# Turning attention rows on VectorE inside the attention instead of on TensorE during the first routing

## The chip, the cores and the metric

The kernel runs on one core of one Trainium2 chip. The metric is the device time of one execution in microseconds (us). The core has five engines that work side by side and wait for one another through semaphores: TensorE (PE in the profile, its weight loads PEld), VectorE (DVE), ScalarE (ACT), GpSimd (POOL) and SyncE (SP), which here only issues transfers (DMAs) and reads a register.

## The reference

An attention with sigmoid in place of softmax, and behind it a mixture of experts in which each token goes to one expert. All inputs are float32.

```python
# q, k, v: (8 batches, 12 heads, 448 tokens, 64)
scores = scale * np.matmul(q, k.transpose(0, 1, 3, 2)) - np.log(S)
attn = 1.0 / (1.0 + np.exp(-scores))
out = np.matmul(attn, v)
# x: (3584 tokens, 768): the heads of a token side by side
x = np.ascontiguousarray(out.transpose(0, 2, 1, 3)).reshape(B * S, H * D)
# experts: N=3584, D=768, E=8, F=1024, cap = N // E = 448 tokens each
logits = x @ w_gate
flat = logits.flatten()
for idx in np.argsort(-flat):                 # best (token, expert) first
    tok, e = (int(idx) // E, int(idx) % E)
    if assigned[tok] >= 0 or counts[e] >= cap:
        continue
    assigned[tok] = e
    counts[e] += 1
    ...
for e in range(E):
    h = np.maximum(x[assigned == e] @ w1[e], 0.0)
    out[assigned == e] = h @ w2[e]
```

## The kernel before

**Attention.** The work is cut into 48 pairs of heads, `(b, pr)` with 8 batches of `NP` = 6 pairs. One turn of the main loop takes a current pair, prepares the next and finishes the old one, and the order of the code is the order on each engine's queue:

1. In every even turn `load` issues the DMAs of two pairs, the fourth and fifth ahead: k and v on SP's queue, q on POOL's. The tiles `nkq` have four buffers, so a load waits until an older tile was turned.
2. `turn(nxt)` (L408) makes `kqT` on VectorE with a transpose of 32x32 blocks (128x896 elements); `split` copies it to `kqH` on ScalarE (L416) and takes the rest `kqL` on VectorE (L417).
3. `scores` (L433) runs on TensorE in three pieces `c`, each followed by a sigmoid on ScalarE (L423) into `at`. The split stands behind the first of the three.
4. `av(old)` (L457, and L463 for odd pairs) multiplies by v on TensorE into PSUM tiles `tp`, of which there are two. VectorE copies the result into `xt` (L465), for odd pairs with an addition (L467). An odd pair takes both `tp` tiles.
5. In even turns `rest_scores` (L443) handles the last 64 tokens of the next pair and the current one.
6. One item of the list `bg` is done: `logits(b)` (L478, TensorE, with an addition on VectorE, L480), or a piece of `rows`.

`XT[b]` holds a batch's attention output with the features on partitions: partition p of pair r is feature 128r + p, and the 448 tokens lie along the free dimension. The experts need whole token rows in the DRAM tensor `xs`, because a token's row is gathered by index. `rows(b, c, hf, eng)` makes them: for 112 tokens and three pairs it does three TensorE transposes into a `tp` tile (L489), copies that to `xr` on ScalarE (L492) or VectorE (L494), and with the second half stores 112 rows of 3072 bytes through SP (L496). A batch takes eight calls. Batch 0's calls go through `bg` during the attention; those of the last `LATE` = 7 batches go to the list `late`, and so `XT` has seven buffers.

**First routing.** Eight times, one expert after the other takes its 448 tokens (`Router.phase`): `keys` on VectorE, a `search` in 16 steps for the threshold, then `pick`, `place` and `lists`. In the first routing a step of the search counts on VectorE (L178), sums over partitions with one small TensorE matmul (L190), and makes the next thresholds on VectorE (L202, L215, L217). Nothing of the experts can run before this routing has picked the first expert and listed its tokens. Between its steps the code puts the late rows: one call before `R.start`, seven behind `keys`, three behind each step of the search. Then `actx.close()` releases the attention's SBUF.

**Experts.** For expert kx, `gather` fetches the tokens' rows from `xs` by an indirect DMA of POOL (L625), `xturn` transposes them on TensorE in blocks of 128 tokens and 128 features (L639: the rows are the stationary operand, the identity streams), and ScalarE and VectorE split them into `xh` and `xl` (L642, L643). Every expert has 24 such transposes, in eight groups of three. Weights come through SP (L592, L596) and are split into `wh` and `wl`; the products are done in three matmuls each (L734 to L738 and L771 to L775). The other routings run beside the experts' matmuls. The experts with kx of 6 and 7 load some weights with a step of two elements (`slice(d2, 256, 2)`, L764) and turn their results on VectorE (L669).

Of the kernel before, what the change touches and what calls it, by code (L numbers as in the profile page):

```python
# [7 lines left out]
F32 = mybir.dt.float32  # L8
# [11 lines left out]
BIG = 16384.0  # L20
TWO23 = float(2 ** 23)
XR_BUFS = 12
LATE = 7
XT_BUFS = 7
XA_BUFS = 5
AT_BUFS = 8
YT_BUFS = 3
# [312 lines left out]
def moe_attention(tc, q, k, v, w_gate, w1, w2, out):  # L340
    nc = tc.nc
    B, H, S, D = q.shape
    DM = H * D
    E, _, F = w1.shape
    CP, NCH, NP, ND, NF = 112, S // 112, H // 2, DM // 128, F // 128
    G4 = 4
    PSUM = bass.MemoryType.PSUM
    with contextlib.ExitStack() as ctx:
# [10 lines left out]
        xa = actx.enter_context(tc.tile_pool(name="xa", bufs=1))  # L359

        xs = dr.tile([B * S, DM], F32, name="xs")
# [9 lines left out]
        def load(b, g, qq=(nc.gpsimd, nc.gpsimd), vq=nc.sync):  # L371


            nat["v", b, g] = ld.tile([128, G4, 3, D], F32, name="nv", bufs=3)
            nat["r", b, g] = ld.tile([128, 2, D], F32, name="nr", bufs=3)
            for i in range(2):
                t = nat["kq", b, 2 * g + i] = ld.tile([128, 2, S // 32, 32], F32, name="nkq", bufs=4)
                for n, (qn, src) in enumerate(((nc.sync, k), (qq[i], q))):
                    for j in range(2):
                        rws = src[b, g * G4 + 2 * i + j].rearrange("(c p) (x d) -> x p c d", p=32, x=2)  # L380
                        for x in range(2):
                            o = 64 * j + 32 * x
                            qn.dma_start(t[o:o + 32, n], rws[x])  # L383
            vs = v[b, g * G4:(g + 1) * G4]
            for h in range(G4):
                vq.dma_start(nat["v", b, g][:, h], vs[h, :384].rearrange("(c p) d -> p c d", p=128))
            for i in range(2):
                vq.dma_start(nat["r", b, g][HI if i == 0 else LO],
                             vs[2 * i:2 * i + 2, 384:].rearrange("h p d -> p h d"))
# [56 lines left out]
        XT = {}  # L446

        def av(b, pr, end=False):


            if pr == 0:
                XT[b] = xa.tile([128, NP, S], F32, name="xt", bufs=XT_BUFS)
            p = ps_t.tile([128, 512], F32, name="tp")
# [18 lines left out]
        def logits(b, prs):  # L472

            s, g = b % 4, b // 4
            p = ps_t.tile([128, 512], F32, name="tp")
            for pr in prs:
                for c in range(NCH):
                    nc.tensor.matmul(p[32 * c:32 * c + 32, :CP], wgz[:, pr, s, :], XT[b][:, pr, c * CP:(c + 1) * CP],  # L478
                                     start=(pr == prs[0]), stop=(pr == prs[-1]))
            nc.vector.tensor_tensor(LE[:, g], LE[:, g], p[:, :CP], OP.add)  # L480

        XR = {}

        def rows(b, c, hf, eng):
            if hf == 0:
                XR[b] = xa.tile([CP, DM], F32, name="xr", bufs=XA_BUFS)
            p = ps_t.tile([128, 512], F32, name="tp")
            for i in range(3):
                nc.tensor.transpose(p[:CP, i * 128:(i + 1) * 128], XT[b][:, hf * 3 + i, c * CP:(c + 1) * CP], ident)  # L489
            dst = XR[b][:, hf * 384:(hf + 1) * 384]  # L490
            if eng == "act":
                nc.scalar.copy(dst, p[:CP, :384])  # L492
            else:
                nc.vector.tensor_copy(dst, p[:CP, :384])  # L494
            if hf == 1:
                nc.sync.dma_start(xs[b * S + c * CP:b * S + (c + 1) * CP], XR[b])  # L496

        pairs = [(b, pr) for b in range(B) for pr in range(NP)]
        NPR = len(pairs)
        turn(*pairs[0], ((0, 1), (1, 2)))()  # L500
        bg, late = [], []
        consts = route_consts(nc, cp, K)
        for i in range(NPR + 1):
            cur = pairs[i] if i < NPR else None
            nxt = pairs[i + 1] if i + 1 < NPR else None
            old = pairs[i - 1] if i else None
            if cur and cur[1] % 2 == 0:
                nx = i // 2 + 2
                if nx < NPR // 2:
                    load(nx // 3, nx % 3)  # L510
            split = turn(*nxt) if nxt else None
            for c in range(3 if cur else 0):
                scores(*cur, c)
                if c == 0 and split:
                    split()
            if bg and not cur:
                bg.pop(0)()
            if old:
                av(*old, not cur)
            if cur and cur[1] % 2 == 0:  # L520
                rest_scores(*nxt)
            if i > 2:
                next(consts, None)
            if bg and cur:
                bg.pop(0)()
            if old == (B - 1, NP - 2):
                bg.append(lambda: logits(B - 1, range(NP - 2)))
            if old and old[1] == NP - 1:
                b = old[0]
                if b < B - 1:  # L530
                    bg.append(lambda b=b: logits(b, range(NP)))
                for c in range(NCH):
                    for hf in range(2):
                        if b >= B - LATE:
                            late.append(lambda b=b, c=c, hf=hf: rows(b, c, hf, "act"))
                        else:
                            bg.append(lambda b=b, c=c, hf=hf: rows(b, c, hf, "dve"))
        for f in bg:
            f()
        logits(B - 1, [NP - 2, NP - 1])  # L540
# [76 lines left out]
        xg, XH = {}, {}  # L617
# [10 lines left out]
        def xturn(kx, j, n, hf, wide):  # L628
            if (j, hf) == (0, 0):
                XH[kx] = (xp.tile([128, ND, S], F32R, name="xh", bufs=2),  # L630
                          xp.tile([128, ND, S], F32R, name="xl", bufs=2))
            xh, xl = XH[kx]
            if wide and hf:
                p = ps_s.tile([128, 2, 512], F32, name="sc")[:, 0]
            else:
                p = ps_t.tile([128, 512], F32, name="tp")
            for i in range(3):
                dd = hf * 3 + i
                nc.tensor.transpose(p[:, i * n:(i + 1) * n], xg[kx, j][:n, dd * 128:(dd + 1) * 128], ident[:n, :n])  # L639
            pv = p[:, :3 * n].rearrange("p (a t) -> p a t", a=3)  # L640
            sl = (slice(None), slice(hf * 3, hf * 3 + 3), slice(j * 128, j * 128 + n))
            nc.scalar.activation(xh[sl], pv, AF.Copy)  # L642
            nc.vector.tensor_tensor(xl[sl], pv, xh[sl].bitcast(F32), OP.subtract)  # L643
# [172 lines left out]
        for kx in range(E):  # L816
# [21 lines left out]
            for step, cost in enumerate(moe(kx)):  # L838
                clock[0] += cost
                t = clock[0]  # L840
# [7 lines left out]
                if t >= t_chore:  # L848
                    c = next((c for c in chores if c[0] <= t), None)
# [37 lines left out]
```

## Time and profile before

| what | value |
|---|---|
| median of 3 runs | 882.02 us (881.35 to 885.34) |
| profiled execution, its own time | 883.43 us |
| its span | 881.7 us |
| mean granted TensorE clock | 0.987 |
| attention (to about 277 us) | TensorE busy throughout from 44 us on |
| first routing (277 to about 320 us) | VectorE busy 35.5 of 43 us, TensorE 30.8 |
| experts (340 to 870 us) | TensorE busy 524 of 530 us |

A line of a group of instructions reads: code line, engine, operation, output<-inputs, shape, number; then busy microseconds in all, mean nanoseconds of one, and the idle time of the engine just before them with what ended it. A line of the chain of waits reads: start, duration, engine, tile, line. A line of a timeline reads: start, duration, engine, line, operation, and in brackets the engine's idle time before it and who ended that. A line of a windows table gives the stretch, its width, the busy time of each engine shown with the number of instructions, the granted clock, the share of the DMA engines and GB/s.

### The profile page before, as it was taken

What the parts mean: (1) busy time and instruction counts of PE and PEld (TensorE: products, weight loads), DVE (VectorE), ACT (ScalarE), POOL (GpSimd) and SP (SyncE); (2) the same over time, 40 slices, a digit from 0 to 9 for tenths busy, and PEclk for the clock granted to TensorE, in tenths of its full rate; (3) what the DMA queues carried; (4) which work ended last, traced back from release to release, by engine and by line L of the source; (5) the groups of instructions that cost most, each with busy time, mean ns of one, the idle gap of its engine ahead of it and who ended that gap; (6) DMA issues with size and microseconds to landing.
All of it is one profiled execution on the core that took longest, in us unless ns stands there. A gap on an engine that the chain in (4) does not pass through costs nothing.

```text
span 881.7 us, 16211 instructions
## 1 busy us (share of the span) xinstructions
PE 840.1 (95%) x5467; PEld 636.9 (72%) x5467; DVE 542.4 (62%) x2060; ACT 447.3 (51%) x612; POOL 466.0 (53%) x446
## 2 busy tenths in 40 slices
PE   6999999999999739998999999999999999999996
PEld 3455555555554528987988988988888888999996
DVE  4566555555554988958859879779779631332130
ACT  6777677777775734434434434534434344541420
POOL 9744344444410014854864873873883883851561
PEclk9999999999999979998999999999999999999999
DMA  9866766666621855443442442551542542634643
GB/s 173 165 142 149 153 126 127 127 126 127 126 43 54 270 192 154 120 138 123 128 136 97 160 155 81 177 162 57 189 153 72 170 153 90 209 96 141 203 151 126
DMA packets 213811, 122.16 MB, mean 139 GB/s; under 512 B 153344, under 2 KB 202496, under 8 KB 213728
## 3 DMA queue, kind: packets, MB, share of 16 engines
q1 hardware_dynamic: 200992, 87.62, 38.2%
q0 software_dynamic: 10880, 33.28, 12.0%
q8 instruction: 43, 0.70, 0.3%
q10 hardware_dynamic: 1856, 0.23, 0.2%
q14 instruction: 40, 0.33, 0.1%
HBM read 96.76 MB, written 24.31 MB: 137 GB/s over the span
## 4 chain that ended last, share of the span: by engine, by line
PE 82%; DVE 11%; issue 2%; DMA 2%; POOL 1%; SPq 1%; ACT 1%; POOLq 0%; DVEq 0%; ACTq 0%
PE tp L457 13%; PE sc L433 11%; PE sc L736 9%; PE sc L734 9%; PE sc L738 9%; PE sc L773 6%; PE sc L775 6%; PE sc L771 6%; DVE r_junk L178 4%; PE tp L463 2%; PE sc L443 2%; PE tp L639 2%; PE tp L652 2%; PE tp L478 1%; PE rt L289 1%
## 5 line engine op out<-in xcount | busy, mean ns | idle before, releaser
L605 POOL TENSOR_TENSOR wl<-wr,wh 128x768 fp32r<-128x768 f32 (+1 forms) x96 | 204.9, 2145 | 124.5 <-ACT wh L603 116.8
L423 ACT ACTIVATE at<-sc,bias 128x896 f32<-128x896 f32 x168 | 161.5, 1006 | 67.1 <-PE sc L443 38.4
L383 POOL DMA_DIRECT2D nkq<-in_q_dram x188 | 118.4, 646 | 116.2 <-DVE kqT L408 104.6
L775 PE MATMUL sc<-hh,wl 128*128 128x448 f32 (+2 forms) x400 | 150.2, 375 | 0.0
L738 PE MATMUL sc<-xh,wl 128*128 128x448 f32 (+2 forms) x396 | 146.2, 369 | 0.0
L736 PE MATMUL sc<-xl,wh 128*128 128x448 f32 (+2 forms) x396 | 146.0, 369 | 0.1
L773 PE MATMUL sc<-hl,wh 128*128 128x448 f32 (+2 forms) x400 | 145.5, 364 | 0.2 <-POOL hl L746 0.2
L734 PE MATMUL sc<-xh,wh 128*128 128x448 f32 (+2 forms) x396 | 145.0, 366 | 0.0
L771 PE MATMUL sc<-hh,wh 128*128 128x448 f32 (+2 forms) x400 | 144.1, 360 | 0.4 <-issue 0.4
L178 DVE TENSOR_SCALAR_CACHE_REDUCE r_junk<-r_KE,r_T 128x224 bf16<-128x224 f32 x315 | 123.2, 441 | 0.1
L603 ACT ACTIVATE wh<-wr 128x768 fp32r<-128x768 f32 (+1 forms) x112 | 102.0, 939 | 36.3 <-DMA wr<-in_moe_w_dram 23.4
L457 PE MATMUL tp<-at,nv 128*64 128x448 f32 x576 | 118.8, 548 | 0.0
L746 POOL TENSOR_TENSOR hl<-yt,hh 128x896 fp32r<-128x896 f32 x32 | 68.4, 2136 | 48.8 <-ACT yt L745 47.2
L742 ACT ACTIVATE hh<-sc 128x896 fp32r<-128x896 f32 x32 | 29.5, 921 | 117.1 <-PE sc L738 117.1
L417 DVE TENSOR_TENSOR kqL<-kqT,kqH 128x896 fp32r<-128x896 f32 (+1 forms) x49 | 52.5, 1073 | 58.5 <-ACT kqH L416 58.4
L773 PEld LDWEIGHTS sc<-hl,wh 128*128 128x128 f32 x400 | 75.8, 189 | 6.8 <-issue 1.1
L625 POOL DMA_INDIRECT xr<-xs,r_idx x32 | 32.0, 999 | 91.2 <-ACT wh L603 80.2
L736 PEld LDWEIGHTS sc<-xl,wh 128*128 128x128 f32 x396 | 75.2, 190 | 6.7 <-issue 0.5
L457 PEld LDWEIGHTS tp<-at,nv 128*64 128x64 f32 x576 | 37.1, 136 | 59.1 <-issue 56.6
L734 PEld LDWEIGHTS sc<-xh,wh 128*128 128x128 f32 x396 | 75.2, 190 | 6.0
L771 PEld LDWEIGHTS sc<-hh,wh 128*128 128x128 f32 x400 | 76.0, 190 | 4.8 <-issue 0.6
L738 PEld LDWEIGHTS sc<-xh,wl 128*128 128x128 f32 x396 | 75.1, 190 | 5.3
(166 smaller groups left out, 1266.1 us busy)
## 6 DMA issues: line engine op xcount, KB each, us to landing
wr<-in_moe_w_dram SPq DMA_DIRECT2D x64, 384.0 KB, 3.0
wr<-in_moe_w_dram SPq DMA_DIRECT2D x48, 512.0 KB, 3.6
nkq<-in_k_dram SPq DMA_DIRECT2D x192, 56.0 KB, 2.6
xs<-xr SPq DMA_DIRECT2D x32, 336.0 KB, 3.3
nkq<-in_q_dram POOLq DMA_DIRECT2D x188, 56.0 KB, 2.7
nv<-in_v_dram SPq DMA_DIRECT2D x92, 96.0 KB, 2.7
ys<-yt SPq DMA_DIRECT2D x20, 112.0 KB, 1.9
nr<-in_v_dram SPq DMA_DIRECT2D x46, 32.0 KB, 2.2
```

The costliest lines, as they stand in the source:

```text
L178: nc.vector.tensor_scalar(junk, KE, T[:, i:i + 1].bitcast(F32), None, OP.is_ge, OP.add, accum_out=cnt[:, i:i + 1])
L383: qn.dma_start(t[o:o + 32, n], rws[x])
L423: nc.scalar.activation(a, p[:, :, :S], AF.Sigmoid, bias=bias, scale=1 / math.sqrt(D))
L457: nc.tensor.matmul(p[j * 64:j * 64 + 64, :S], nat["v", b, g][:, h0 + j, c, :], AT[b, pr, c][:, j, :], start=(c == 0), stop=(c == 2 and pr ...
L603: nc.scalar.activation(hi, raw[u], AF.Copy)
L605: eng.tensor_tensor(lo, raw[u], hi.bitcast(F32), OP.subtract)
L734: nc.tensor.matmul(ph[:, f, lo:hi], wh[:, a, fs], xh[:, dd, lo:hi], start=st, stop=False)
L736: nc.tensor.matmul(ph[:, f, lo:hi], wh[:, a, fs], xl[:, dd, lo:hi], start=False, stop=False)
L738: nc.tensor.matmul(ph[:, f, lo:hi], wl[:, a, fs], xh[:, dd, lo:hi], start=False, stop=en)
L771: nc.tensor.matmul(py[:, d2, :w], wh[:, a, dsl], h1, start=st, stop=False)
L773: nc.tensor.matmul(py[:, d2, :w], wh[:, a, dsl], h2, start=False, stop=False)
L775: nc.tensor.matmul(py[:, d2, :w], wl[:, a, dsl], h1, start=False, stop=(j == 1 and a == 3))
```

## The change

- `rows` is now used for the last batch alone (`LATE` = 1): eight calls, one before `R.start` and seven behind `keys`; nothing is put between the steps of the search any more. Batch 0's rows leave the attention as well.
- A new function `turn_rows` does batches 0 to 6. After each odd pair an item goes into `bg` that transposes two pairs (128x896 elements) in blocks of 32x32 on VectorE, in one instruction. Three such items make a batch, 21 in all; the logits of a batch come behind the third. Its output `xz` is [128, 14, 32, 6]: the six pairs lie innermost, so the instruction writes with a step of six elements (24 bytes).
- With the third item SP stores the batch in four DMAs, one for 32 partitions, each of 32x14 pieces of 192 elements (768 bytes). A row of `xs` now holds feature 128r + p at column 6p + r.
- `rows` writes its copy on ScalarE with the same step of six, so that batch 7 has that order too.
- `xturn` takes the columns `dd::NP`, every sixth element of a gathered row, as the stationary operand of its transposes.
- `XT` has three buffers in place of seven; `xz` has two.

```diff
-LATE = 7
-XT_BUFS = 7
+LATE = 1
+XT_BUFS = 3
+XZ_BUFS = 2
...
-        def rows(b, c, hf, eng):
+        def rows(b, c, hf):
...
-            dst = XR[b][:, hf * 384:(hf + 1) * 384]
-            if eng == "act":
-                nc.scalar.copy(dst, p[:CP, :384])
-            else:
-                nc.vector.tensor_copy(dst, p[:CP, :384])
+            dst = XR[b].rearrange("p (c r) -> p r c", r=NP)[:, hf * 3:hf * 3 + 3]
+            nc.scalar.copy(dst, p[:CP, :384].rearrange("p (r c) -> p r c", r=3))
...
+        def turn_rows(b, pr):
+
+            if pr == 1:
+                XR[b] = xa.tile([128, S // 32, 32, NP], F32, name="xz", bufs=XZ_BUFS)
+            nc.vector.transpose(XR[b].rearrange("p i j r -> p r i j")[:, pr - 1:pr + 1],
+                                XT[b][:, pr - 1:pr + 1].rearrange("p r (i t) -> p r i t", t=32))
+            if pr == NP - 1:
+                for a in range(4):
+                    nc.sync.dma_start(xs[b * S:(b + 1) * S, 192 * a:192 * a + 192].rearrange("(i t) c -> t i c", t=32),
+                                      XR[b][32 * a:32 * a + 32].rearrange("t i j r -> t i (j r)"))
...
+            if old and old[1] % 2 and old[0] < B - LATE:
+                bg.append(lambda b=old[0], pr=old[1]: turn_rows(b, pr))
             if old and old[1] == NP - 1:
                 b = old[0]
                 if b < B - 1:
                     bg.append(lambda b=b: logits(b, range(NP)))
-                for c in range(NCH):
+                for c in range(NCH if b >= B - LATE else 0):
                     for hf in range(2):
-                        if b >= B - LATE:
-                            late.append(lambda b=b, c=c, hf=hf: rows(b, c, hf, "act"))
-                        else:
-                            bg.append(lambda b=b, c=c, hf=hf: rows(b, c, hf, "dve"))
+                        late.append(lambda b=b, c=c, hf=hf: rows(b, c, hf))
...
-                nc.tensor.transpose(p[:, i * n:(i + 1) * n], xg[kx, j][:n, dd * 128:(dd + 1) * 128], ident[:n, :n])
+                nc.tensor.transpose(p[:, i * n:(i + 1) * n], xg[kx, j][:n, dd::NP], ident[:n, :n])
```

## The prediction, made before the changed kernel ran

> **What bounds the kernel now.** I read the page's first part, then a table of windows by stage, then the chain of waits and the timeline inside the stages that the change touches.
>
> ```profile
> PE 840.1 (95%) x5467; PEld 636.9 (72%) x5467; DVE 542.4 (62%) x2060; ACT 447.3 (51%) x612; POOL 466.0 (53%) x446
> ...
> 44.00:105.00 61.00, 61.00 (x520) 32.16 (x514) 38.06 (x70) 42.94 (x47) 25.09 (x40) 1.00 0.72 150
> 105.00:277.00 172.00, 172.00 (x1450) 86.91 (x1450) 92.23 (x112) 125.88 (x138) 65.26 (x104) 1.00 0.52 106
> 277.00:320.00 43.00, 30.75 (x216) 19.23 (x216) 35.48 (x202) 26.50 (x57) 0.00 (x0) 0.99 0.70 225
> 340.00:870.00 530.00, 524.29 (x2913) 466.29 (x2912) 338.02 (x1605) 213.01 (x320) 325.82 (x211) 0.99 0.43 135
> ```
>
> The window rows give, after the width, the busy time of PE, PEld, DVE, ACT and POOL, then the granted clock, the DMA share and GB/s. The attention (to 277 us) and the experts (from 340) are bound by TensorE, which is busy for the whole of two windows and 524 of 530 us of the other. The first routing (277 to 320) is not: there VectorE is busy 35.5 of 43 us. So a microsecond taken off TensorE counts in the attention and in the experts, and in the routing only if the row work there stands in VectorE's way. The profiled execution took 883.43 us, span 881.7; the median of the three timed runs is 882.02, 1.4 us less.
>
> **The row transposes that go.** By windows of line 489 alone (PE and PEld busy), and by the chain:
>
> ```profile
> 44.00:105.00 61.00, 4.31 (x24) 2.36 (x24) 1.00 0.72 150
> 276.00:320.00 44.00, 27.52 (x168) 16.74 (x168) 0.99 0.68 220
> by line: PE tp L457 39.4%; PE sc L433 35.3%; PE tp L463 7.5%; PE sc L443 7.4%; PE tp L489 6.6%; PE tp L478 4.3%
> ```
>
> Batch 0's 24 transposes run between 44 and 105 us, and the third row is the chain of that window: L489 is 6.6% of 61 us, 4.0 us, all on the path. **Term 1: -4.0 us.** Batch 0's eight VectorE copies (L494) go too, off the path.
>
> The other 168 run in the routing; 24 of them (batch 7) stay. The 144 that go, with 48 ACT copies, look large. The chain there:
>
> ```profile
> 290.71 0.04 issue
> 290.75 0.18 PE rt L190
> ...
> 290.95 0.18 DVE r_j L202 x2
> ...
> 291.15 0.16 DVE r_T L215
> 291.31 0.13 DVE r_J L217
> 291.44 1.11 DVE r_junk L178 x6
> ...
>   DVE r_j L202: 0.5, 2
> ```
>
> One search step takes 1.85 us, nearly all VectorE. Its TensorE instruction starts 0.04 us after the last count although row transposes stand around it in PE's queue; over 16 steps r_j waited for it 0.5 us in all (last row). So taking the late rows away gives the search nothing: term 0. (The stores that these rows feed: next fence.)
>
> **What the routing may lose.** With no row work TensorE idles through the search:
>
> ```profile
> 316.00:318.00 2.00, 0.00 (x0) 0.00 (x0) 1.79 (x7) 0.00 (x0) 0.00 (x0) 1.00 0.73 240
> 318.00:320.00 2.00, 0.59 (x3) 0.35 (x3) 1.46 (x9) 0.00 (x0) 0.00 (x0) 0.78 0.02 6
> 320.00:322.00 2.00, 0.00 (x0) 0.10 (x1) 1.90 (x5) 0.00 (x0) 0.00 (x0) 0.50 0.45 151
> L190 PE MATMUL rt<-r_cnt,c_G x16: 164/164/164, 286.4 to 314.8; 128*128 128x3 bf16 x16
> L167 PE MATMUL rt<-ident,r_KT x14: 257/269/368, 284.1 to 648.7; 112*128 112x112 f32 x14
> ```
>
> The last two columns, DMA share and GB/s, show the late stores through by 318 us (240 GB/s, then 6), before the first weights start: they hold up nothing either. The granted clock is still 1.00 just after the row transposes and 0.50 from 320. After the change it should fall near 290. L167's slowest against its usual, 368 to 269 ns, is my bound for a cold matmul, 1.4 times; so L190 may cost up to 66 ns more, 16 times: 0 to +1.1 us. **Term 2: +0.5.** The Trainium skill (TensorE: Matmul & The Clock Gate, Part 4) says that transposes do not count as busy for the clock, so that it would be low here already and this term zero; the 1.00 above, with little but transposes on PE, speaks against it. By its formulas for a single matmul (same page, Single matmul latency) a cold L190 is 185 ns for 167 warm, an estimate of 0.3 us over 16.
>
> Batch 7's eight ACT copies now write every sixth element. In the chain three of them (0.49 us each) alternate with transposes ahead of the keys' transpose:
>
> ```profile
> 282.52 0.49 ACT xr L492
> 283.06 1.04 PE tp L489 x6
> 284.13 0.42 PE rt L167 x2
> ```
>
> Free if such writes cost nothing; at 1.68 times the streaming part (below) some 0.2 us each, over five or six copies about 1.2. **Term 3: +0.4**, nearer the free end: no scattered ACT write is in the trace.
>
> **The turn on VectorE.** 21 block transposes of 128x896, three a batch, each right after an even pair's xt copy and ahead of the next kqT:
>
> ```profile
> L408 DVE STREAM_TRANSPOSE kqT<-nkq 128x896 f32<-128x896 f32 x47 | 51.8, 1103 | 2.5 <-DMA nv<-in_v_dram 1.5 <-DMA nkq<-in_k_dram 0.2
> L408 DVE STREAM_TRANSPOSE kqT<-nkq 128x448 f32<-128x448 f32 x2 | 1.2, 624 | 5.7 <-DMA nkq<-in_k_dram 5.7
> L669 DVE STREAM_TRANSPOSE yt<-sc 128x896 f32<-128x896 f32 x5 | 5.6, 1118 | 32.5 <-PE sc L775 25.0 <-issue 7.5
> L151 DVE TENSOR_REDUCE rt<-ML 112x32 f32<-112x256 f32 x7 | 4.2, 605 | 0.2
> 175.06 1.10 DVE L408 STREAM_TRANSPOSE kqT<-nkq 128x896 f32<-128x896 f32 x1
> 177.23 1.09 DVE L417 TENSOR_TENSOR kqL<-kqT,kqH 128x896 fp32r<-128x896 f32 x1 [1.08 <-ACT kqH L416]
> 179.87 0.62 DVE L465 COPY xt<-tp 128x448 f32<-128x448 f32 x1 [1.55 <-PE tp L463]
> 180.71 1.91 ACT L423 ACTIVATE at<-sc,bias 128x896 f32<-128x896 f32 x2 [1.71 <-PE sc L443]
> ```
>
> The first two rows make a transpose 145 ns and 1.07 ns per element. L669, the same operation writing every second element (8 bytes apart), takes 1118. The new one writes 24 bytes apart, a step that no row has. L151 reads SBUF at 64 bytes apart: (605-145)/256 = 1.80 ns per element, 1.68 times the dense rate. So one turn costs 1.1 to 145+896x1.80 = 1760 ns. Its cover is the idle time behind the delayed kqT: VectorE idles 1.55 us before the odd pair's copy, ACT 1.71 us before the next sigmoid but one. All of 1.1 hides and 1.76 nearly; without that cover 21 turns would cost 23 to 37 us. I take 1.1 to 1.2, since L669 is nearest. What queues behind a turn: kqT, then kqH and two sigmoids on ACT, then scores of the next pair. The logits of batches 0 to 6 move one pair later, behind an odd pair that uses both tp banks, so they wait for that copy (0.62 us, in the fence): 0 to 7 x 0.62 = 4.3 us. TensorE has the next pair's rest scores to do meanwhile, so I take a tenth: **term 4: +0.5**.
>
> **DMA.** Batch by batch, four stores of 32x14 pieces of 768 bytes replace four of 112 of 3072: the same 336 KB and the same count of 32 in all, 28 now inside the attention. A batch's 1.4 MB in 33 us is 42 GB/s; at the routing's 225 GB/s for a share of 0.70 that adds 0.13 to the attention's 0.52 to 0.72, or 0.26 if smaller pieces halve the rate.
>
> ```profile
> SPq L496 <- DVE xr L494: 10.3, 4, 3.3
> nkq<-in_k_dram SPq DMA_DIRECT2D x112, 56.0 KB, 2.5
> ```
>
> On SP the next k and v loads queue behind a store that waits for the turn. Batch 0's four stores did just that (10.3 us of SP waiting) and PE showed no gap from 44 to 105 us; loads land 2.5 us after issue, and the code issues them for the fourth and fifth pair ahead. POOL's q loads and gathers pass nothing. Zero; without the lead each store wait would cost up to 3.3 us, seven times.
>
> **The experts' transposes.** All 192 now load their stationary operand at a step of 24 bytes:
>
> ```profile
> 340.00:870.00 530.00, 26.69 (x168) 19.30 (x168) 0.99 0.43 135
> L639 PEld LDWEIGHTS tp<-ident,xr 128*128 128x128 f32 x135 | 16.9, 144 | 15.0 <-DVE xl L643 6.5 <-issue 5.1 <-DMA xr<-xs,r_idx 0.9
> L478 PEld LDWEIGHTS tp<-xt,wgz 128*32 128x32 f32 x384 | 8.9, 110 | 7.3 <-DVE kqL L417 3.5 <-ACT xt L465 1.6 <-issue 1.4
> L771 PEld LDWEIGHTS sc<-hh,wh x97: 186/188/192, 399.8 to 543.6; 128*128 128x128 f32 x97
> L771 PEld LDWEIGHTS sc<-hh,wh x62: 193/194/195, 782.7 to 849.7; 128*128 128x128 f32 x62
> 526.26 0.49 PE L639 MATMUL tp<-ident,xr 128*128 128x128 f32 x3
> 526.51 0.45 PE L773 MATMUL sc<-hl,wh 128*128 128x448 f32 x1
> ```
>
> Three transposes take 526.26 to 526.51, 83 ns apart, so the load of the next sets their pace; the first of a group loads under the matmul before it. Two are exposed per group, 64 groups. Low end: L771, dense in the middle experts and every second element in the last two, goes from 188 to 194 ns: +6 x 128 = 0.8 us. High end: L151's 1.80 ns for all 128 columns, 230 ns in place of 83: 64 x (2x147+25) = 20 us. Between: 32 columns load in 110 ns and 128 in 144, so some 45 ns stream; 1.68 times that is +31 ns, 128 x 31 = 3.9. I take it, since 24 bytes lies between 8 and 64. **Term 5: +3.9.**
>
> The Trainium skill (Advanced Engine Details and Errata, Memory Cachelines) says that SBUF is read in lines of 16 bytes and needs two hits per line for full speed. L669's and L771's 8 bytes, nearly free, and L151's 64, dear, agree; by it 24 bytes pays in full, and at half speed for the streamed 45 ns term 5 would be 5.8 us, an estimate.
>
> **Sum** on the profiled 883.4: -4.0 + 0.5 + 0.4 + 0.5 + 3.9 = +1.3; on the median, 883.
>
> **Rivals.**
> - The strided load goes at L151's rate, and TensorE becomes slower in all experts: 883 - 3.9 + 20 = 899 at the end. It decides from 57 ns more per load (128 x 57 = 7.3 us), where the total passes 886.4. For: L151; the experts are all PE. Against: L771's 6 ns. Chance 0.22.
> - Strides are free: 883 less 3 to 4, 879 to 880. For: L771, L669. Chance 0.28.
> - The turn outgrows its cover: at 2.2 us, (2.2-1.71) x 21 = 10 us, 893; any time over 1.9 shows. For: nothing measured writes 24 bytes apart. Chance 0.10.
> - The late rows do hold something back that the chain hides (stores in the way of the first weights or the gather), so that the routing shortens by 2 to 3 us: 876 to 877.5. Against: the 0.04 us above. Chance 0.08.
>
> **Numbers.** The sum's own case has 0.32 (880.5 to 886.4 as terms 2 to 5 vary). About 0.5%, 4.4 us, is what a measurement can tell from no change. Faster is the last rival, 0.08; slower the first and third and an edge of my own case, 0.34; the same 0.58. The range 877 to 896 leaves out half the last rival and the far ends of the slower two.
>
> **What would show it.** Right: L489 gone from 44 to 277 us with about 4 us off the attention's end; turns near 1.1 us and PE still full; search steps still 1.85 to 1.9; L639's weight loads near 170 ns. Wrong: gaps before L433 after each turn, kqT waiting for nkq, search steps shorter, or L639 still at 144 or over 200 ns.

## The result and the profile after

| | before | after |
|---|---|---|
| median (lowest to highest) | 882.02 us (880.60 to 885.34, 5 runs) | 887.13 us (885.73 to 887.36, 5 runs) |
| ratio to before, with its 95% interval | 1 | 1.0051 [1.0028, 1.0074] |
| profiled execution, its span | 883.43 us, 881.7 us | 887.19 us, 885.4 us |
| mean granted TensorE clock | 0.987 | 0.965 |

The change makes the kernel about half a per cent slower: 4.5 us, with an interval from 2.5 to 6.5, on the very bound between no change and slower that the forecast had drawn. The forecast was 883 within 877 to 896. The losses and gains that the experiments below trace to single steps add up to 2.3 to 2.8 us, near the low end of that interval. That they are the whole loss is not shown.

The page's first line and the windows of the same stages (busy time of PE, PEld, DVE, ACT and POOL, then the granted clock, the DMA share and GB/s), after:

```profile
PE 822.1 (93%) x5299; PEld 630.3 (71%) x5299; DVE 572.0 (65%) x2073; ACT 428.8 (48%) x564; POOL 465.7 (53%) x446
```

```profile
44.00:105.00 61.00, 60.42 (x512) 30.59 (x506) 44.01 (x69) 46.45 (x52) 28.11 (x45) 1.00 0.77 168
105.00:277.00 172.00, 170.72 (x1452) 86.06 (x1448) 113.89 (x127) 125.55 (x136) 63.31 (x101) 1.00 0.70 149
277.00:320.00 43.00, 8.37 (x48) 5.00 (x48) 35.82 (x204) 5.96 (x8) 0.00 (x0) 0.59 0.11 33
340.00:870.00 530.00, 525.35 (x2886) 471.24 (x2886) 337.74 (x1606) 212.48 (x319) 325.56 (x211) 0.99 0.43 134
```

TensorE has 18.0 us less work in all (840.1 to 822.1) and 22.4 less in the routing's stage alone (30.75 to 8.37), and the kernel is not faster: in that stage VectorE is busy for 35.8 of 43 us, as before. The attention is a little less full than before (60.42 of 61 us; it was 61.00), which suggests that the turns are not wholly hidden. The second stretch shows 170.72 of 172, but its last two microseconds are already past the attention's end. In the experts' window TensorE is as full as before (525.35 and 524.29 of 530 us), so what grew there should show in the time.

The groups of instructions that the change touches, after, with the ordinary dense transpose (L409) for comparison. The columns behind the bar are busy us in all, mean ns of one, and idle time before them:

```profile
L501 DVE STREAM_TRANSPOSE xz<-xt 128x896 f32<-128x896 f32 x21 | 38.9, 1852 | 0.0
L409 DVE STREAM_TRANSPOSE kqT<-nkq 128x896 f32<-128x896 f32 x47 | 51.6, 1097 | 3.4 <-DMA nv<-in_v_dram 2.2 <-DMA nkq<-in_k_dram 0.5
L648 PEld LDWEIGHTS tp<-ident,xr 128*128 128x128 f32 x135 | 24.3, 223 | 11.2 <-issue 5.1 <-DVE xl L652 4.3 <-DMA xr<-xs,r_idx 0.9
L493 ACT COPY xr<-tp 112x384 f32<-112x384 f32 x8 | 6.0, 856 | 1.8 <-PE tp L491 1.8
```

Each operation that steps by 24 bytes became dearer: the turn takes 1852 ns where the dense transpose of the same size takes 1097, the weight load 223 where it took 144, the ScalarE copy 856 (it was 0.49 us in the chain of before).

Where the time went is best seen between fixed points of the program. Two lines give them: the 24 additions that finish odd pairs (L467 before, L468 after: the first and the last start bracket the attention), and the 28 activations of experts 1 to 7 (L742 and L751). In a row the three numbers are the shortest, median and longest duration in ns, and then come the first and last start. Before, then after:

```profile
L467 DVE TENSOR_TENSOR xt<-tp,xt x24: 614/614/625, 23.2 to 277.9; 128x448 f32<-128x448 f32 x24
L742 ACT ACTIVATE hh<-sc x28: 918/921/922, 416.8 to 842.1; 128x896 fp32r<-128x896 f32 x28
```

```profile
L468 DVE TENSOR_TENSOR xt<-tp,xt x24: 614/615/624, 23.4 to 275.4; 128x448 f32<-128x448 f32 x24
L751 ACT ACTIVATE hh<-sc x28: 918/920/922, 416.9 to 845.9; 128x896 fp32r<-128x896 f32 x28
```

The attention takes 252.0 us for 254.7: it gains 2.7. Experts 1 to 7 take 429.0 for 425.3: they lose 3.7. In between another microsecond goes, which the chain shows, after:

```profile
275.41 0.61 DVE xt L468
...
277.14 0.55 PE tp L491 x3
277.76 4.51 ACT xr L493 x6
...
283.09 0.40 DVE r_KE L171
```

From the last addition's start to the keys' copy it is 7.68 us (275.41 to 283.09); before it was 6.62 (277.96 to 284.58). In the chain six copies by ScalarE now follow one another without TensorE between them; before, the chain alternated between the two.

These three stretches make +2.1 of the 3.7 us by which the two spans differ (885.4 and 881.7). The other 1.6 lie between the keys' copy and the first activation of expert 1: 132.2 us before (284.58 to 416.8) and 133.8 after (283.09 to 416.9). But in the profiles of all twelve kernels, the experiments' included, this stretch took between 129.6 and 134.1 us, with dense and strided loads mixed, so one pair of profiles can't tell what the change costs there.

### The profile page after: what moved, and what is told of

Read it like the earlier page. It is cut to its first block, busy times and chain, and to the rows that moved or that the text cites. A ratio compares the mean times of both kernels' runs of the same rounds, so it can differ in the third digit from the quotient of the medians.

```text
span 885.4 us, 15786 instructions
## 1 busy us (share of the span) xinstructions
PE 822.1 (93%) x5299; PEld 630.3 (71%) x5299; DVE 572.0 (65%) x2073; ACT 428.8 (48%) x564; POOL 465.7 (53%) x446
## 4 chain that ended last, share of the span: by engine, by line
PE 79%; DVE 11%; DMA 3%; issue 3%; ACT 2%; SPq 1%; POOL 1%; DVEq 0%; ACTq 0%; POOLq 0%
PE tp L458 10%; PE sc L745 9%; PE sc L743 9%; PE sc L434 9%; PE sc L747 9%; PE sc L782 7%; PE sc L784 7%; PE sc L780 7%; DVE r_junk L179 3%; PE tp L648 3%; PE tp L464 2%; PE tp L661 2%; PE sc L444 1%; PE tp L479 1%; DMA nv<-in_v_dram 1%
## 5 line engine op out<-in xcount | busy, mean ns | idle before, releaser
L751 ACT ACTIVATE hh<-sc 128x896 fp32r<-128x896 f32 x32 | 29.5, 920 | 116.4 <-PE sc L747 116.4
L784 PEld LDWEIGHTS sc<-hh,wl 128*128 128x128 f32 x400 | 76.6, 192 | 4.2
```

Of the source, the lines that this page charges most:

```text
L784: nc.tensor.matmul(py[:, d2, :w], wl[:, a, dsl], h1, start=False, stop=(j == 1 and a == 3))
```

## The experiments

**e1_dense_load: the changed kernel with the dense weight load.**

```diff
-nc.tensor.transpose(p[:, i * n:(i + 1) * n], xg[kx, j][:n, dd::NP], ident[:n, :n])
+nc.tensor.transpose(p[:, i * n:(i + 1) * n], xg[kx, j][:n, dd * 128:(dd + 1) * 128], ident[:n, :n])
```

> The changed kernel, but the experts' transposes take 128 neighbouring columns again as stationary operand (the features then reach the experts in another order than w1 has, so the output differs). Step theory: the step of 24 bytes in the weight load is what costs in the experts: loads back from 223 to 144 ns, the last expert's first relu 5 us earlier against the first expert's, the first expert's start 1 to 2 us earlier, 880 to 881 us in all, ratio to before 0.998 to 0.999. Rival, the moved stores or the other layout of SBUF slow the run: loads fast again but the time stays at 886 to 887.

Measured: 881.89 us, ratio 0.998 [0.9966, 0.9994]. Its load group and its activations:

```profile
L648 PEld LDWEIGHTS tp<-ident,xr 128*128 128x128 f32 x135 | 16.9, 144 | 15.2 <-DVE xl L652 6.5 <-issue 5.3 <-DMA xr<-xs,r_idx 0.9
```

```profile
L751 ACT ACTIVATE hh<-sc x28: 917/919/923, 415.4 to 840.5; 128x896 fp32r<-128x896 f32 x28
```

The load is back at 144 ns and experts 1 to 7 at 425.1 us. Without this one step in the load the changed kernel is a little faster than before.

**e2_before_strided_load: the kernel before with the strided load**, the same line turned the other way round.

> The kernel before with one edit: the experts' transposes take every sixth column (rows stay in natural order, so the output differs). Step theory: the experts lose 5 us and the first expert's start 1 to 2, 888 to 889 us, ratio 1.007 to 1.008, with loads of 223 ns. Rival: loads at 223 ns are hidden and nothing moves, 882 us.

Measured: 887.65 us, ratio 1.005 [1.0032, 1.0067], so 2.8 to 5.9 us slower.

```profile
L639 PEld LDWEIGHTS tp<-ident,xr 128*128 128x128 f32 x135 | 24.2, 223 | 11.4 <-issue 5.3 <-DVE xl L643 4.4 <-DMA xr<-xs,r_idx 0.9
```

```profile
L742 ACT ACTIVATE hh<-sc x28: 917/919/923, 416.6 to 845.5; 128x896 fp32r<-128x896 f32 x28
```

428.9 us for seven experts, 3.6 more than before: the load by itself makes the whole loss of the experts, with nothing of the change in the attention.

What a slower load costs in a group of three transposes, in the timeline of TensorE (start, duration, line; the row below the transposes is the next matmul). After, then e1:

```profile
526.76 0.54 PE L648 MATMUL tp<-ident,xr 128*128 128x128 f32 x3
527.06 0.45 PE L782 MATMUL sc<-hl,wh 128*128 128x448 f32 x1
```

```profile
524.82 0.49 PE L648 MATMUL tp<-ident,xr 128*128 128x128 f32 x3
525.06 0.45 PE L782 MATMUL sc<-hl,wh 128*128 128x448 f32 x1
```

A group takes 0.30 us in place of 0.24. Over the 48 groups of experts 1 to 7 that stand by themselves in each trace the medians are 298 and 246 ns: the load grew by 80 ns, but two exposed loads make such a group only some 50 ns longer. Some groups lose more, since 3.7 us over 56 groups are 66 ns each.

**e3_dense_act: the changed kernel, batch 7's copies dense.**

```diff
-dst = XR[b].rearrange("p (c r) -> p r c", r=NP)[:, hf * 3:hf * 3 + 3]
-nc.scalar.copy(dst, p[:CP, :384].rearrange("p (r c) -> p r c", r=3))
+nc.scalar.copy(XR[b][:, hf * 384:(hf + 1) * 384], p[:CP, :384])
```

> The changed kernel with batch 7's ScalarE copies dense again (batch 7's columns then lie in another order than the experts read). Step theory: the eight copies go from 856 to 480 ns, and the search starts 1.1 us earlier behind the end of the attention (7.6 us instead of 8.6 us); the whole run gains up to that, 886 us. Rival, the keys on VectorE set the start: the copies shorten and the search starts when it did, 887 us.

Measured: 885.08 us, ratio 1.0017 [1.0004, 1.0031]. Its chain at the same place:

```profile
275.61 0.62 DVE xt L468
...
277.96 0.49 ACT xr L492
...
278.49 0.56 PE tp L491 x3
```

The copies take 0.49 us again and alternate with transposes. From the last addition to the keys' copy it is 6.6 us, as before: the scattered copies cost 1.06 us.

**e4_dense_turn: the changed kernel, the turn writing side by side.**

```diff
-XR[b] = xa.tile([128, S // 32, 32, NP], F32, name="xz", bufs=XZ_BUFS)
-nc.vector.transpose(XR[b].rearrange("p i j r -> p r i j")[:, pr - 1:pr + 1],
+XR[b] = xa.tile([128, S // 32, NP, 32], F32, name="xz", bufs=XZ_BUFS)
+nc.vector.transpose(XR[b].rearrange("p i r j -> p r i j")[:, pr - 1:pr + 1],
...
-    XR[b][32 * a:32 * a + 32].rearrange("t i j r -> t i (j r)"))
+    XR[b][32 * a:32 * a + 32].rearrange("t i r j -> t i (r j)"))
```

> The changed kernel with the turn writing blocks of 32 neighbouring elements; the stores and their pieces of 768 bytes stay (the columns then lie in another order than the experts read). Step theory: the turn goes from 1852 to about 1100 ns; its cover holds both, so all pairs of heads from batch 2 on keep their spacing of 6.16 and 4.43 us and only the start of batch 1 gains, 0.3 to 0.6 us in all, 886.5 us. Rival, the longer turn holds TensorE up in the attention: the attention ends 1.4 us earlier or more, 885.5 us or less.

Measured: 885.14 us, ratio 1.0018 [1.0006, 1.0031].

```profile
L501 DVE STREAM_TRANSPOSE xz<-xt 128x896 f32<-128x896 f32 x21 | 23.1, 1101 | 0.0
```

```profile
L468 DVE TENSOR_TENSOR xt<-tp,xt x24: 612/616/625, 22.8 to 273.7; 128x448 f32<-128x448 f32 x24
```

The turn takes 1101 ns and the attention 250.9 us: 1.1 less than after, 3.8 less than before. So the part of a 1852 ns turn that its cover does not hide is 1.1 us in all, over 21 turns. The dense turn seems to be hidden whole: all pairs of e4 without logits but the first keep the spacing of 4.43 and 6.16 us that before's have outside batch 0's row calls. Pair by pair in the trace (counted from 1, from the start of one pair's multiplication by v to the next), the changed kernel is longer than e4 by 0.24, 0.43 and 0.18 us at pairs 6, 8 and 10, and by 0.03 to 0.06 at each of the other six logits slots.

**e8_consts_later: what stands in the way at pairs 6, 8 and 10.** VectorE also makes the routing's constants there (L113), a few in each turn of the loop from the third on. The experiment lets them begin at the twenty-first.

```diff
-            if i > 2:
+            if i > 20:
```

> The changed kernel with the routing's small constant instructions on VectorE made from turn 21 of the main loop on in place of turn 3. Theory: the 0.2 to 0.5 us that the pairs 6, 8 and 10 lose against the spacing of 6.16 and 7.50 us come from these instructions together with the turn; they go there, and reappear at the pairs 24 to 30; the time stays at 886 to 887. Rival, the loads are late in this early part because of the stores: the pairs 6, 8 and 10 keep their loss.

Measured: 885.61 us in one run, with these additions:

```profile
L468 DVE TENSOR_TENSOR xt<-tp,xt x24: 610/615/626, 23.2 to 275.1; 128x448 f32<-128x448 f32 x24
```

The three losses vanish from pairs 6, 8 and 10 and stand at pairs 24, 26 and 28 (0.22, 0.41 and 0.17 us); the attention is as long as after, 251.9 us. So here the turn loses where it meets other work of VectorE on top of its own queue, and moving that work moved the loss without making it smaller.

**e7_turn_twice: how deep is the cover?** Each turn is done twice in a row.

```diff
-nc.vector.transpose(XR[b]..., XT[b]...)
+for _ in range(2):
+    nc.vector.transpose(XR[b]..., XT[b]...)
```

> The changed kernel with every turn done twice, 3.7 us of VectorE in place of 1.85. Theory of the cover (1.7 to 1.9 us behind a delayed kqT): about 1.8 us more for each of 21 turns, 35 us, 915 to 925 us, with gaps of TensorE ahead of the scores. Rival, VectorE's idle time takes it all (it is busy about 66% in the attention): under 892 us.

Measured: 921.97 us in one run, 34.8 more than after.

```profile
L502 DVE STREAM_TRANSPOSE xz<-xt 128x896 f32<-128x896 f32 x42 | 76.3, 1816 | 0.7
```

```profile
L468 DVE TENSOR_TENSOR xt<-tp,xt x24: 612/615/624, 23.2 to 311.5; 128x448 f32<-128x448 f32 x24
```

The attention takes 288.3 us, 36.3 more: 1.73 us for each second turn, which lasts 1.82. Nearly nothing of it is hidden. The cover is therefore about 1.9 us (twice 1.82, less 1.73): the single turn of 1.85 fills it to the brim. Pair by pair, and against e4, it is some 2.0 us where a turn stands alone and some 1.8 beside the logits (two turns make the pair 1.66 and 1.87 us longer there), which fits the few hundredths that the single turn loses at the logits slots alone.

**e6_warm: the clock in the search.** The changed kernel with 48 spare row calls (transposes and dense copies whose results nobody reads) put back between the steps of the search.

```diff
+def spare(c, hf):
...
+if b >= B - LATE:
+    for n in range(48):
+        late.append(lambda n=n: spare(n // 2 % NCH, n % 2))
```

> The changed kernel with 48 spare row calls put back between the steps of the search (transposes of batch 7 and dense ScalarE copies to a scratch tile, no stores). Theory of the prediction: the search does not feel them, 1.85 us a step with and without; the clock stays at 1.00 to 315 us, which gives back 0.1 to 0.4 us of cold matmuls; 886 to 887 us. Rival, the late rows did hold the routing back: steps of 1.9 us or more and 1 to 3 us longer.

Measured: 885.56 us, ratio 1.0024 [1.0011, 1.0036]. The counting matmuls of the search, after and then in e6:

```profile
L191 PE MATMUL rt<-r_cnt,c_G x16: 164/164/188, 284.9 to 313.3; 128*128 128x3 bf16 x16
```

```profile
L191 PE MATMUL rt<-r_cnt,c_G x16: 164/164/164, 284.8 to 313.2; 128*128 128x3 bf16 x16
```

The windows of the search in e6, and in the changed kernel:

```profile
277.00:300.00 23.00, 18.28 (x117) 11.54 (x118) 18.71 (x102) 18.18 (x34) 0.00 (x0) 1.00 0.19 61
300.00:318.00 18.00, 12.17 (x76) 7.25 (x74) 15.46 (x96) 10.29 (x22) 0.00 (x0) 0.98 0.01 2
```

```profile
277.00:300.00 23.00, 5.85 (x36) 3.65 (x37) 18.69 (x104) 5.96 (x8) 0.00 (x0) 0.66 0.19 61
300.00:318.00 18.00, 2.51 (x12) 1.35 (x11) 15.35 (x94) 0.00 (x0) 0.00 (x0) 0.50 0.00 0
```

The spare work keeps the clock at 1.00 and 0.98 in the two stretches, against 0.66 and 0.50 without it, and the search gains nothing: 28.4 us from the first count to the last in both, with counting matmuls of 164 ns at the median in both. The few small matmuls behind the search are what a cold clock makes longer: in the trace it is 39.9 us from the keys' copy to the first expert's list of tokens after, 39.7 in e6 and 39.6 before, so 0.2 to 0.3 us.

**e5_pairs: a step of 8 bytes in place of 24.** Features lie in twos instead of sixes: the turn and batch 7's copies write every second element, a batch is stored in twelve transfers of 256-byte pieces, and the experts load every second column. `xz` has three buffers here and in e9.

```diff
-XR[b] = xa.tile([128, S // 32, 32, NP], F32, name="xz", bufs=XZ_BUFS)
+z = xa.tile([128, S // 32, 32, 2], F32, name="xz", bufs=XZ_BUFS)
...
-nc.tensor.transpose(p[:, i * n:(i + 1) * n], xg[kx, j][:n, dd::NP], ident[:n, :n])
+nc.tensor.transpose(p[:, i * n:(i + 1) * n], xg[kx, j][:n, 256 * (dd // 2) + dd % 2:256 * (dd // 2) + 256:2], ident[:n, :n])
```

> The change in another layout, complete and in the experts' order: a turn writes two pairs of heads side by side (step of 8 bytes), batch 7's ScalarE copies and the experts' weight loads have the same step of 8 bytes, and every turn stores at once in four DMAs of 448 pieces of 256 bytes (twelve a batch in place of four of 768-byte pieces). Step theory: turn about 1.12 us, loads 140 to 150 ns, the search 6.0 to 6.3 us behind the attention's end; the attention keeps the gain of batch 0's rows, 3 to 4 us, and the experts lose nothing: 879 us, ratio 0.995 to 0.997. Rival, the pieces: three times as many issues on SP and smaller pieces make the k and v loads late, kqT waits for nkq, and the attention gives the gain back: 883 or more.

Measured: 884.08 us, ratio 1.001 [0.9999, 1.0021].

```profile
L501 DVE STREAM_TRANSPOSE xz<-xt 128x896 f32<-128x896 f32 x21 | 23.1, 1102 | 0.0
L648 PEld LDWEIGHTS tp<-ident,xr 128*128 128x128 f32 x135 | 22.2, 203 | 12.6 <-DVE xl L652 5.7 <-issue 5.3 <-DMA xr<-xs,r_idx 0.7
```

```profile
L751 ACT ACTIVATE hh<-sc x28: 917/918/923, 413.2 to 840.7; 128x896 fp32r<-128x896 f32 x28
```

The expected gain did not come. For VectorE 8 bytes are free (1102 ns, dense 1101). For TensorE's load they are not: 203 ns, and experts 1 to 7 take 427.5 us, 2.2 more than before. With 0.3 us for the copies (6.94 us from the last addition to the keys' copy), the cold clock and an attention 3.9 us shorter, these terms make about -1.1 us, where the runs show +0.9 (-0.1 to +1.9). The one trace is of the second fastest of twelve executions (882.13 us) and does not show where the rest goes.

**e10_steps: the load alone, by step.** The kernel before, with steps of 4, 4, 8, 12, 16, 20, 24 and 4 bytes for experts 0 to 7.

```diff
+STEPS = (1, 1, 2, 3, 4, 5, 6, 1)
...
-nc.tensor.transpose(p[:, i * n:(i + 1) * n], xg[kx, j][:n, dd * 128:(dd + 1) * 128], ident[:n, :n])
+nc.tensor.transpose(p[:, i * n:(i + 1) * n], xg[kx, j][:n, STEPS[kx] * 0 + min(dd, DM - 127 * STEPS[kx] - 1):][:, :127 * STEPS[kx] + 1:STEPS[kx]], ident[:n, :n])
```

> The kernel before, with the stationary operand of the experts' transposes read at a step that goes by the expert: 4, 4, 8, 12, 16, 20, 24 and 4 bytes for experts 0 to 7 (other columns than the reference's are turned in experts 2 to 6, so the output differs). It measures the load by itself at each step. Theory A (a price by lines of 16 bytes, two hits on a line at full speed): about 140 ns at 4 and 8 bytes, dearer at 12, and one price, about 225, from 16 on. Theory B (any step beyond 4 bytes breaks the load's full speed, as the 205 ns at 8 bytes of the version in pairs suggests): about 205 at 8 bytes and 205 to 230 from 12 to 24. Theory C (it grows with the bytes that a step spans): a rise by equal amounts, about 157 at 8, 174 at 12, 191 at 16, 208 at 20, 225 at 24. The time as a whole: 884 to 886 us.

Measured: 882.18 us in one run, under the forecast of 884 to 886. One answer of the trace for each of experts 1 to 6 (a window over a part of their transposes, shortest, median and longest load):

```profile
L640 PEld LDWEIGHTS tp<-ident,xr x15: 135/139/144, 401.6 to 405.2; 128*128 128x128 f32 x9, 64*128 64x128 f32 x6
L640 PEld LDWEIGHTS tp<-ident,xr x9: 191/213/219, 469.1 to 472.6; 64*128 64x128 f32 x6, 128*128 128x128 f32 x3
L640 PEld LDWEIGHTS tp<-ident,xr x3: 189/208/209, 536.1 to 536.3; 64*128 64x128 f32 x3
L640 PEld LDWEIGHTS tp<-ident,xr x6: 192/214/216, 599.9 to 602.0; 64*128 64x128 f32 x6
L640 PEld LDWEIGHTS tp<-ident,xr x6: 188/209/213, 668.1 to 670.2; 64*128 64x128 f32 x6
L640 PEld LDWEIGHTS tp<-ident,xr x9: 206/235/239, 730.2 to 734.3; 64*128 64x128 f32 x6, 128*128 128x128 f32 x3
```

Over all 24 loads of an expert the medians are 140, 200, 196, 201 and 200 ns at 4, 8, 12, 16 and 20 bytes, and 212 at 24. That is theory B: one price of about 60 ns for the steps from 8 to 20 bytes, nothing that happens at 16, and a little more at 24. Theories A and C both fail at 8 bytes. Experts 1 to 7, five of them with a step, take 1.6 us more than before (426.9 for 425.3):

```profile
L743 ACT ACTIVATE hh<-sc x28: 917/920/922, 413.9 to 840.8; 128x896 fp32r<-128x896 f32 x28
```

The single time is lower than before's all the same; the last section shows how much one run can vary there.

**e9_dense_all: the turn on VectorE, and no step anywhere.** The order of the columns is chosen so that the turn and batch 7's copies write side by side and the load reads side by side. The stores sort the columns with finer pieces (twelve transfers a batch), and the first weights are loaded in four transfers of 32 partitions, in the same order.

```diff
-XR[b] = xa.tile([128, S // 32, 32, NP], F32, name="xz", bufs=XZ_BUFS)
+z = xa.tile([128, S // 32, 2, 32], F32, name="xz", bufs=XZ_BUFS)
...
+o = 384 * (a // 2) + 128 * (pr // 2) + 64 * (a % 2)
+nc.sync.dma_start(xs[b * S:(b + 1) * S, o:o + 64].rearrange("(i t) c -> t i c", t=32), ...)
...
+src = w1[ds(gate[kx], 1)].rearrange("x (g e h l p) f -> e h l p (x g) f", g=3, e=2, h=2, l=2, p=32)
+for q in range(4):
+    nc.sync.dma_start(t[32 * q:32 * q + 32], src[q % 2, j, q // 2][:, :, i * 256:(i + 1) * 256])
```

> The complete kernel, with the changed one's turn by VectorE kept, and every 24-byte step taken out: the turn writes runs that lie side by side, batch 7's copies by ScalarE write side by side, the stores put the columns in their places by finer pieces, and the first weights are loaded in the matching order of rows, four transfers for each unit in place of one. Theory (the loss is the 24-byte steps, the gain is batch 0's): a turn of 1.10 us, copies of 0.48 us, weight loads of 140 ns; about 1.1 us less in the attention, 1.0 less between the attention's end and the search and 5 less in the experts than the changed kernel, so 879.5 to 880.5 us, a ratio of 0.996 to 0.998. Rival (the order costs elsewhere what the steps cost): more issues on SyncE, or first weights that come late in four pieces, give back 2 us or more: 882 us and above, with idle time behind the first weights' transfers or behind the stores.

Measured: 880.54 us, ratio 0.9974 [0.9962, 0.9987]: faster than before by 2.3 us (1.1 to 3.4), and the lowest median of the kernels timed here, though e1's ratio lies within its interval.

```profile
L501 DVE STREAM_TRANSPOSE xz<-xt 128x896 f32<-128x896 f32 x21 | 23.1, 1101 | 0.0
L649 PEld LDWEIGHTS tp<-ident,xr 128*128 128x128 f32 x135 | 17.2, 146 | 15.4 <-DVE xl L653 6.5 <-issue 5.3 <-DMA xr<-xs,r_idx 1.1
L492 ACT COPY xr<-tp 112x384 f32<-112x384 f32 x8 | 3.8, 479 | 2.3 <-PE tp L491 1.8
```

```profile
L468 DVE TENSOR_TENSOR xt<-tp,xt x24: 614/616/625, 23.1 to 274.0; 128x448 f32<-128x448 f32 x24
L752 ACT ACTIVATE hh<-sc x28: 918/920/923, 414.7 to 839.9; 128x896 fp32r<-128x896 f32 x28
```

```profile
wr<-in_moe_w_dram SPq DMA_DIRECT2D x256, 96.0 KB, 2.2
```

Attention 250.9 us, experts 1 to 7 425.2, and the first weights' 256 transfers take 2.2 us each from issue to landing. Each of the three losses is gone, but of the 3.8 us gained in the attention only 2.3 reach the time. The cold clock takes 0.2 to 0.3 of the difference. The rival of costs elsewhere may have come in part: behind the keys' copy the first two splits of weights by ScalarE start after 39.8 and 41.2 us, for 39.0 and 39.7 in e1, the second gather starts 0.4 us later, and from the last activation to the end it is 40.0 us for 39.6. No run here takes these apart.

## Why the prediction was right or wrong

The forecast's time was 4 us too low and its range held the result. The sign of the sum was right (+1.3 forecast, +2.3 to +2.8 by the terms below, +4.5 by the direct comparison). That last gap stays open within the interval. With the terms that an experiment takes away put back, four of them point to its low end: e1's -1.8 us and 4.2 make +2.4, e3's +1.5 and 1.06 make +2.6, e4's +1.6 and 1.1 make +2.7, and e6's +2.1 with 0.2 to 0.3 for the clock makes +2.4. Two point to its middle: e9's -2.3 makes +4.1 with the three losses put back, and e5's +0.9 makes +4.5 with what it saves of them (1.1, 0.8 and 1.7).

| step of the forecast | forecast, us | by the runs, us |
|---|---|---|
| 1, batch 0's transposes leave the attention | -4.0 | -3.8 (e4, e9: 250.9 for 254.7) |
| the turn beyond its cover, and term 4 | 0 and +0.5 | +1.1 together |
| 2, cold clock | +0.5 | +0.2 to 0.3 |
| 3, batch 7's scattered copies | +0.4 | +1.06 |
| 5, weight load at a step of 24 bytes | +3.9 | +3.7 in experts 1 to 7, some 4.2 if the first loses as much |

**Terms 1 and 5 carry the result and were right in size.** Term 5 was right for a reason that was only half right, and in part by luck. The step was taken to slow the 45 ns that stream, to 31 ns more; the load itself grew by 80. What counts on the path is the group, and 3.7 us over the 112 exposed loads of seven experts is 33 ns each; the rest of a load seems to lie beside the matmuls around it. That 31 and 33 agree comes from two errors that cancel, a load dearer than forecast and less of it exposed. By the forecast's own signs the load came out wrong (near 170 ns was to be right, over 200 wrong). The first expert is left out of the measured number: its beginning varies by more than the effect (see the last section). The 4.2 only extends the rate of the other seven to it, which is too much: the first expert's first twelve loads run at a granted clock of 0.50 and take 182 to 230 ns even when dense (before), 209 to 240 with the step (after). Only its other twelve, at 1.00 and 0.94, differ by more: 134 to 147 ns dense, 207 to 243 with the step.

**The turn was mis-sized, and the cover saved it.** The forecast took 1.1 to 1.2 us, led by L669's 8 bytes, with 1.76 as the high end, and turns near 1.1 us were to be a sign that it was right. The turn is 1.85, above the high end: (1852 - 145) / 896 = 1.91 ns per element, 1.78 times the dense rate, where L151 at 64 bytes had given 1.68. The cover was read as 1.55 to 1.71 us and is about 1.9 (e7). Both were read too low, the turn by some 0.7 us and the cover by 0.2 to 0.35. That only 1.1 us came through, of which the logits slots have 0.3, is luck: a turn of 1.85 us would have overrun the cover that was read, 1.71 at most, by 0.14 or more each time, 3 us in all. The claim that a time over 1.9 would show is what e7 bears out.

**Term 4 was right in sign and had the wrong cause.** The logits slot costs the pair 1.30 us before (5.73 for 4.43) and 1.34 after (7.50 for 6.16), as it moved from an even to an odd pair; with the dense turn it is 1.28. So its new place costs nothing by itself, and the little that it costs belongs to the long turn.

**Term 3 was the worst mis-sized.** It was taken near its free end, because no scattered ScalarE write stood in the trace; the copies grew from 478 to 856 ns, a factor of 1.79, and 1.06 us reached the path, near the high end of 1.2 that L151's rate had given. The row at 64 bytes was a better guide to 24 bytes than the rows at 8.

**The zeros held.** The search is unchanged: 28.4 us from its first count to its last, before (286.4 to 314.8) and after (284.9 to 313.3). Nor does the first expert's list come earlier behind the keys' copy (39.9 us after, 39.6 before), so the rival in which the late rows held the routing back is refuted. The seven batches' stores inside the attention cost nothing that shows in the spacing of e4's pairs, which have the same stores, although one issue of four takes SyncE 4 us:

```profile
52.30 4.00 SPq L505 DMA_DIRECT2D xs<-xz  x4
```

**The rule on cache lines.** By the Trainium skill (Advanced Engine Details and Errata, Memory Cachelines) two hits on a line of 16 bytes give full speed. VectorE's writes agree at both steps: 8 bytes 1102 ns, 24 bytes 1852. TensorE's load here does not: it pays at 8 bytes already and no more at 16 or 20 (e10), so the measurement decides. The forecast had taken L771's 6 ns at 8 bytes for a sign that this step is nearly free, and as the low end of term 5; that load, of another tile, takes 188 ns when dense, and it did not stand for one of 144.

**Term 2 and the rule on the clock.** The Trainium skill says that transposes do not count as busy for the clock in the same way as other matmuls (TensorE: Matmul & The Clock Gate, Part 4). The changed kernel, with next to nothing on TensorE, fell to 0.50 in the search, and e6, with little but transposes, held 0.98 to 1.00. The traces go against that sentence, as the forecast supposed. The cold clock cost 0.2 to 0.3 us where 0.5 was taken, but not at the place that was forecast: the counting matmuls, which were to take up to 66 ns more, stayed at 164 ns at the median, and the loss stands in the few matmuls behind the search.

## What to carry to other kernels

A change of layout has to be followed to each place where it is read and written: here three operations on three engines paid for one step of 24 bytes, together some 6 us (5.9 to 6.4) against 3.8 won. Work moved into another engine's idle time is worth only what the idle time holds: measure that depth by doubling the moved work before relying on it. Where a step between elements can't be avoided, put it into the transfers: e9 moved it from the engines into finer DMA pieces, whose stores left the attention at 250.9 us, and turned the loss into a gain.

## What the runs showed of the hardware that was not expected

- The stationary operand of TensorE's float32 transposes loads in about 200 ns instead of 140 when it is read at a step of 8, 12, 16 or 20 bytes, and in 212 to 223 at 24 (e10, after). VectorE's transpose writes at 8 bytes for nothing (1102 ns) and at 24 for 1852.
- A cold clock slows the dense load but hardly the one with a step: 182 to 230 ns against 134 to 147 for the dense one (the first expert before, at a granted clock of 0.50 and then 1.00), and 209 to 240 against 207 to 243 at 24 bytes (after, at 0.50 and then 0.94).
- When the clock comes back behind the routing differs from profile to profile, even where the program is the same. Windows at the start of the first expert, before, after, in e2 (whose search has all the late rows) and in e10 (which does the same work as before up to the end of the first expert, with dense loads there too):

```profile
330.00:336.00 6.00, 5.38 (x36) 4.79 (x34) 4.89 (x16) 3.00 (x6) 0.38 (x4) 0.77 0.91 272
```

```profile
330.00:336.00 6.00, 5.97 (x28) 5.76 (x29) 4.72 (x20) 1.92 (x5) 0.73 (x1) 0.53 0.93 289
```

```profile
330.00:336.00 6.00, 5.48 (x26) 5.13 (x26) 4.65 (x17) 2.39 (x5) 0.82 (x1) 0.54 0.98 298
```

```profile
330.00:336.00 6.00, 5.44 (x29) 4.83 (x28) 4.77 (x17) 2.13 (x5) 0.03 (x1) 0.60 0.82 251
```

The granted clock there is 0.77, 0.53, 0.54 and 0.60, and in the twelve profiles the first expert took 14.4 to 16.4 us from its first transpose to its first activation, dense and strided loads mixed (after 16.4, e9 16.0, e3 14.9, before 14.4). That is nearly as much as the terms' sum, so a single pair of profiles shows the terms and not their sum. That the clock alone makes this difference is not shown.
